# Hand-set order on all engines, eight 64x32 tiles for the state products, a transposed recurrent read and crossbar transposes in a cross-attention and ReGLU kernel

## The chip, the cores and the metric

The kernel runs on one core of a Trainium2 chip (trn2). The metric is the device time of one execution in microseconds (us); each figure is a median of several executions, and lower is better. A profile is one execution; its span, from the first to the last instruction, is about 1.8 us shorter than the time of the same execution.

The engines are called as the profile calls them: PE (matmuls), PEld (its weight loads), DVE (VectorE), ACT (ScalarE), POOL (GpSimd), SP (the engine that issues most DMAs here). "Crossbar transpose" is the name here for a transpose done by a DMA from one SBUF tile to another (DMA_TRANSPOSE in the traces). In these kernels the operands lie in SBUF, and PE leaves its products in PSUM, in pools of one-bank tiles, until ACT or DVE has read them.

## The reference, cut to what matters

Shapes: `x` is 8 batches of 8 heads, 512 tokens, 64 dimensions; `state` is 8 by 8 by 32 by 64. The feed-forward part has d_model 512 and d_ff 1536.

```python
scores = scale * x @ state^T                       # per batch and head: 512 x 32
a      = softmax(scores)                           # over the 32 states
xread  = a @ state                                 # 512 x 64
scores2 = scale * state @ x^T                      # the same products, transposed
a2     = softmax(scores2)                          # over the 512 tokens
sread  = a2 @ x                                    # "recurrent read": 32 x 64
X = concat([xread, sread], tokens).reshape(8 * 544, 512)
out = (relu(X @ w_gate) * (X @ w_val)) @ w_out     # 4352 x 512, float32
```

Both versions use one algebraic step: for the 512 tokens of a batch, `xread @ w_gate` equals `a @ (state @ w_gate)`. The kernel computes `U = state @ w` for each batch (the "state products", for gate and value), and then one "gate product" with the attention as the moving operand. Only 256 rows per batch (8 heads of 32 states) enter the contraction instead of 512.

## The kernel before: the parts that matter

Everything is in bf16 with float32 accumulation. PE's order is set by hand; the other engines are ordered by the scheduler (`engines={PE}`).

```python
ps_gv = pool("ps_gv", 6, PS)      # PSUM banks for state products, gate and value products
ps_o  = pool("ps_o", 1, PS)       # one bank for output products
ps_m  = pool("ps_m", 1, PS)       # one bank for all that attention needs
...
def x_trans_pe(b, j):             # x transposed on PE, 4 x 4 per batch, copied by ACT or DVE
    ps = ps_m.tile([128, NC, 128], BF16, name="xT_ps", tag="m")
    for c in range(NC):
        nc.tensor.transpose(ps[:, c], xb[b][:, c, 2*j:2*j+2]..., id128)
...
def att_sr(b, kc):                # recurrent read: 8 heads x 32 states on the output rows
    ps = ps_m.tile([128, 272], FP32, name="sr_ps", tag="m")
    for c in range(NC):           # every head against every head of the half: 128 x 256
        nc.tensor.matmul(ps[:, 0:256], e_sn[...], xb[...], ...)
        nc.tensor.matmul(ps[:, 256:257], e_sn[...], ones, ...)    # row sums
    rr = 1 / ps[:, 256:257]                                       # DVE, 128 x 1
    for j2 in range(2):           # keep the wanted blocks, scaled (DVE, 64 x 128)
        nc.vector.tensor_scalar_mul(out=sr_sb[...], in0=ps[...], scalar1=rr[...])
def att_srT(b): ...               # and back: two PE transposes, two copies
...
def u_unit(b, w, kc, lo, n):      # state products: two 128x64 tiles side by side
    for j2 in range(2):
        nc.tensor.matmul(ps[64*j2:64*j2+64, 0:n], stT[:, b, 2*kc+j2], wsb[:, 2*kc+j2, lo:lo+n])
...
for s in range(2, B):             # a steady stage: 12 steps
    for jf in range(12):
        gv(s, jf)                 # 4 gate/value products of 512 columns, then ReLU and multiply
        out_mms(...)              # 4 output products of batch s-2
        # at steps 1, 5, 9: a burst of state products for batch s+1
        # at the others: one attention unit of batch s+1
```

`stT` holds two heads' states with zeros in between (a 128x64 block with two 64x32 blocks on its diagonal), so half of each state product multiplies zeros.

The softmax here doesn't subtract the row's maximum and nothing guards it: scores larger than these inputs give would overflow.

## Time and profile before

| | before |
|---|---|
| median time | 289.81 us (289.37 to 290.25, 2 runs) |
| span of the profiled run | 287.0 us |
| PE busy | 249.4 us, 87% |
| first gate product on PE | 27.03 us |
| first ReLU of stage 2 (all batches in steady flow from here) | 80.72 us |
| one of five steady stages | 27.85 us |
| last ReLU of the state rows to the end | 26.6 us |

A useful clock for this kernel is the start of the ReLUs on ACT: there are twelve per batch, so the 25th starts stage 2, and each following dozen is one stage. The "end" line is counted from the last of them.

The page of the kernel before: engine shares, then busy tenths in 40 slices with the clock granted to PE, then the chain of work that ended last.

```profile
span 287.0 us, 4072 instructions
PE 249.4 (87%) x1562; PEld 123.4 (43%) x1584; DVE 159.9 (56%) x289; ACT 123.2 (43%) x231; POOL 23.2 (8%) x32
...
PE   7264968799599999989998999999999999997773
...
PEclk9655889799999999999999999999999999999999
...
PE 71%; DVE 14%; issue 5%; ACT 5%; DMA 3%; SPq 0%; ACTq 0%
```

A warning on the PEclk line, which bears on all pages here: the traces hold no clock event before the first change (6.40 us in this one), and the line shows full clock up to there. The warm-up matmuls start 0.43 us apart in this trace, and matmuls of the same 512 columns start 0.216 us apart where it records a clock of 1.00 (the four from 138.38 on, below), so PE in fact ran at half clock then.

PE is the bound in the middle (slices at 9), and it is not in most of the first dozen slices and in the last four. So there are three questions: how much PE work a stage has, how long the set-up is, and why the end is loose.

The set-up, on PE, in the timeline of before (columns: start, duration, engine, line, what, and in brackets the idle time before it with what released it):

```profile
7.74 0.40 PE L133 MATMUL xT_ps<-id_94,xb 128*128 128x128 bf16 x4 [0.98 <-ACT xb L119]
12.68 0.58 PE L133 MATMUL xT_ps<-id_94,xb 128*128 128x128 bf16 x4 [4.54 <-ACT xT L135]
13.78 0.58 PE L133 MATMUL xT_ps<-id_94,xb 128*128 128x128 bf16 x4 [0.52 <-DVE xT L137]
15.04 0.59 PE L133 MATMUL xT_ps<-id_94,xb 128*128 128x128 bf16 x4 [0.67 <-ACT xT L135]
```

Each group after the first waits for the copy of the group before, because they share the one `ps_m` bank.

A steady stage by engine, in the windows view (busy time and number of instructions; then the clock, the share of the DMA engines and GB/s), between two first ReLUs:

```profile
110.30:138.15 27.85, 27.00 (x176) 13.04 (x178) 18.78 (x33) 14.07 (x26) 2.03 (x2) 1.00 0.16 60
```

PE is busy for 27.00 of 27.85 us at full clock (1.00): only less PE work makes the stage shorter, apart from the 0.85 us that it idles. One burst of state products in it, in the timeline:

```profile
138.38 1.03 PE L252 MATMUL o_ps<-wo_sb,h_sb 128*128 128x512 bf16 x4
139.34 0.62 PE L206 MATMUL up<-wg_sb,stT 128*64 128x512 bf16 x4
139.79 0.60 PE L206 MATMUL up<-wv_sb,stT 128*64 128x512 bf16 x4
140.32 0.40 PE L133 MATMUL xT_ps<-id_94,xb 128*128 128x128 bf16 x4
```

Ends are modelled and matmuls overlap (the first line shows 1.03 us, and the second starts 0.96 us after it), so read starts. Four output products started at 138.38 hold PE for 0.86 us (four times 0.216); the transposes could then have started at 139.24 and started at 140.32. The burst costs 1.08 us.

Most of the idle 0.85 us is one wait, before the attention transposes:

```profile
126.51 1.23 DVE L158 TENSOR_TENSOR a_sn<-e_sn,rc 128x1024 bf16<-128x1024 bf16 x1
...
127.65 0.71 DVE L185 TENSOR_SCALAR sr_sb<-sr_ps,rr 64x128 bf16<-64x128 f32 x2
...
128.41 0.40 PE L165 MATMUL aT_ps<-id_94,a_sn 128*128 128x128 bf16 x4 [0.70 <-DVE sr_sb L185]
```

And the end, where output products alternate with copies out of a single bank:

```profile
262.07 2.75 PE L252 MATMUL o_ps<-wo_sb,h_sb 128*128 128x512 bf16 x11 [0.78 <-DVE o_sb L263]
265.49 2.75 PE L252 MATMUL o_ps<-wo_sb,h_sb 128*128 128x512 bf16 x12 [0.68 <-ACT o_sb L261]
```

### The profile page before, as it was taken

Reading aid. Unit: us, or ns where it says so; the run is one execution under the profiler, and the core shown is the slowest. Engines: PE = TensorE matmul, PEld = TensorE weight load, DVE = VectorE, ACT = ScalarE, POOL = GpSimd, SP = SyncE. Lnnn points to the kernel's source line nnn. Section 1 sums busy time; section 2 is a strip of 40 time slices with the busy share of each in tenths; the row PEclk is TensorE's granted clock in tenths of the full one; section 3 lists DMA queues with packets and bytes.
Section 4 is the critical chain, followed back from the end, with each engine's and each line's share of the span. In section 5 each row is a group of like instructions: output and inputs, shape, how many; then the busy total and the mean of one; then the engine's idle time right before and its main releaser. Section 6 shows DMA issues by size and latency. Waiting matters only on the chain.

```text
span 287.0 us, 4072 instructions
## 1 busy us (share of the span) xinstructions
PE 249.4 (87%) x1562; PEld 123.4 (43%) x1584; DVE 159.9 (56%) x289; ACT 123.2 (43%) x231; POOL 23.2 (8%) x32
## 2 busy tenths in 40 slices
PE   7264968799599999989998999999999999997773
PEld 3142423344244444444444444444445445664331
DVE  3244749477855866686568656765686444222010
ACT  2341746377264545545554555356544442221000
POOL 8302022200110020002000000000000000000000
PEclk9655889799999999999999999999999999999999
DMA  8999943440040115001011011001010011011112
GB/s 191 219 246 216 242 91 130 133 147 0 2 146 37 39 38 184 37 38 39 37 74 39 0 59 53 37 33 43 38 39 37 37 46 67 37 73 39 73 73 74
DMA packets 21235, 22.80 MB, mean 79 GB/s; under 512 B 3040, under 2 KB 16864, under 8 KB 21216
## 3 DMA queue, kind: packets, MB, share of 16 engines
q1 hardware_dynamic: 14176, 17.30, 18.0%
q0 software_dynamic: 5808, 4.72, 10.3%
q10 hardware_dynamic: 1232, 0.52, 0.8%
q8 instruction: 12, 0.20, 0.3%
q14 instruction: 7, 0.06, 0.1%
HBM read 18.35 MB, written 8.91 MB: 95 GB/s over the span
## 4 chain that ended last, share of the span: by engine, by line
PE 71%; DVE 14%; issue 5%; ACT 5%; DMA 3%; SPq 0%; ACTq 0%
PE o_ps L252 27%; PE gv_ps L227 24%; PE up L206 7%; PE gvs_ps L240 4%; PE xT_ps L133 3%; DVE h_sb L232 3%; DMA xf<-in_x_dram 3%; DVE sr_sb L185 2%; PE aT_ps L165 2%; PE sr_ps L176 2%; PE sc_ps L146 2%; DVE a_sn L158 2%; ACT e_sn L148 1%; DVE cs L154 1%; DVE UG L211 1%
## 5 line engine op out<-in xcount | busy, mean ns | idle before, releaser
L252 PE MATMUL o_ps<-wo_sb,h_sb 128*128 128x512 bf16 x363 | 94.0, 379 | 4.0 <-DVE o_sb L263 1.6
L232 DVE TENSOR_TENSOR h_sb<-gv_ps,g_sb 128x512 bf16<-128x512 f32 x96 | 66.2, 691 | 54.4 <-ACT g_sb L231 49.3
L231 ACT ACTIVATE g_sb<-gv_ps 128x512 bf16<-128x512 f32 x96 | 57.4, 598 | 52.6 <-PE gv_ps L227 46.7
L227 PE MATMUL gv_ps<-ans,UG 128*128 128x512 bf16 x192 | 59.3, 390 | 0.3 <-ACT ans L169 0.2
L227 PE MATMUL gv_ps<-ans,UV 128*128 128x512 bf16 x192 | 58.7, 387 | 0.3 <-DVE UV L211 0.3
L252 PEld LDWEIGHTS <-h_sb 128*128 128x128 bf16 x384 | 37.5, 98 | 46.6 <-issue 4.3
L227 PEld LDWEIGHTS <-UV 128*128 128x128 bf16 x192 | 19.0, 99 | 25.3 <-issue 1.8
L123 POOL CAST xb<-xf 128x1024 bf16<-128x1024 f32 x14 | 14.2, 1042 | 107.0 <-PE sr_ps L179 71.9
L209 ACT CAST UG<-up 128x512 bf16<-128x512 f32 (+1 forms) x26 | 14.4, 554 | 19.4 <-PE up L206 19.3
L211 DVE CAST UG<-up 128x512 bf16<-128x512 f32 (+1 forms) x26 | 16.7, 643 | 10.6 <-PE up L206 10.6
L133 PE MATMUL xT_ps<-id_94,xb 128*128 128x128 bf16 x128 | 13.0, 227 | 8.9 <-ACT xT L135 6.6
L227 PEld LDWEIGHTS <-UG 128*128 128x128 bf16 x192 | 15.3, 99 | 9.2 <-issue 2.5
L263 DVE COPY o_sb<-o_ps 128x512 f32<-128x512 f32 x16 | 11.1, 692 | 12.6 <-PE o_ps L252 12.6
L261 ACT COPY o_sb<-o_ps 128x512 f32<-128x512 f32 x16 | 9.4, 586 | 19.4 <-PE o_ps L252 19.4
L133 PEld LDWEIGHTS <-xb 128*128 128x128 bf16 x128 | 9.4, 101 | 17.0 <-issue 11.4
L211 DVE CAST UV<-up 128x512 bf16<-128x512 f32 (+1 forms) x26 | 16.6, 640 | 0.0
L206 PEld LDWEIGHTS <-stT 128*64 128x64 bf16 x208 | 10.4, 115 | 14.2 <-issue 9.4
L206 PE MATMUL up<-wg_sb,stT 128*64 128x512 bf16 (+1 forms) x104 | 16.4, 394 | 0.0
L206 PE MATMUL up<-wv_sb,stT 128*64 128x512 bf16 (+1 forms) x104 | 16.2, 394 | 0.0
L176 PE MATMUL sr_ps<-xb,e_sn 128*128 128x256 bf16 x64 | 11.7, 285 | 4.2 <-DVE sr_sb L185 3.5
L165 PE MATMUL aT_ps<-id_94,a_sn 128*128 128x128 bf16 x64 | 6.7, 231 | 9.5 <-DVE sr_sb L185 7.8
L209 ACT CAST UV<-up 128x512 bf16<-128x512 f32 (+1 forms) x26 | 14.5, 558 | 0.6 <-PE up L206 0.4
(53 smaller groups left out, 183.9 us busy)
## 6 DMA issues: line engine op xcount, KB each, us to landing
out_dram<-o_sb SPq DMA_DIRECT2D x32, 256.0 KB, 2.3
xf<-in_x_dram SPq DMA_DIRECT2D x7, 1024.0 KB, 5.6
wo_sb<-in_moe_w_out_dram POOLq DMA_DIRECT2D x3, 512.0 KB, 24.0
xf<-in_x_dram SPq DMA_DIRECT2D x2, 512.0 KB, 6.9
wg_sb<-in_moe_w_gate_dram POOLq DMA_DIRECT2D x2, 512.0 KB, 15.0
wv_sb<-in_moe_w_val_dram POOLq DMA_DIRECT2D x2, 512.0 KB, 17.8
wg_sb<-in_moe_w_gate_dram POOLq DMA_DIRECT2D x2, 256.0 KB, 8.3
wv_sb<-in_moe_w_val_dram POOLq DMA_DIRECT2D x2, 256.0 KB, 8.9
```

Source lines behind the costliest of these rows:

```text
L123: nc.gpsimd.tensor_copy(out=o, in_=s)
L133: nc.tensor.transpose(ps[:, c], xb[b][:, c, 2 * j:2 * j + 2].rearrange("p h d -> p (h d)"), id128)
L165: nc.tensor.transpose(ps[:, c], asn[b][:, c, 128 * kc:128 * kc + 128], id128)
L176: nc.tensor.matmul(ps[:, 0:256], e_sn[b][:, c, 4 * kc:4 * kc + 4].rearrange("p h n -> p (h n)"), xb[b][:, c, 4 * kc:4 * kc + 4].rearrange( ...
L206: nc.tensor.matmul(ps[64 * j2:64 * j2 + 64, 0:n], stT[:, b, 2 * kc + j2], wsb[:, 2 * kc + j2, lo:lo + n], start=True, stop=True)
L209: nc.scalar.copy(out=usb[:, kc, lo:lo + n], in_=ps[:, 0:n])
L211: nc.vector.tensor_copy(out=usb[:, kc, lo:lo + n], in_=ps[:, 0:n])
L227: nc.tensor.matmul(ps.rearrange("p (c t) -> p c t", c=NC), usb[:, kc, f0:f0 + 128], ANS[b][:, :, kc], start=(kc == 0), stop=(kc == 1))
L231: nc.scalar.activation(out=g_sb, in_=pss[0], func=AF.Relu)
L232: nc.vector.tensor_tensor(out=hsb[b][:, jf], in0=pss[1], in1=g_sb, op=ALU.mult)
L240: nc.tensor.matmul(ps[:, w], wsb[:, j, f0:f0 + 128], br[:, j].rearrange("p b n -> p (b n)"), start=(j == 0), stop=(j == NJ - 1))
L252: nc.tensor.matmul(o_ps[0], src[:, jf, tsub * 128:(tsub + 1) * 128], wo_sb[:, jf], start=(jf == 0), stop=(jf == NF - 1))
```

## The change

Its intent: take transposes and zeros off PE, and order all engines so that PE rarely waits. In parts:

1. **State products on eight 64x32 tiles.** The diagonal blocks of `stT` are multiplied alone, two row groups by four column groups of the array, meant to take the time of the zeros away (0.40 us per burst in E1). The state is put into this form by products with permutation matrices (`perm`) instead of transposes.
2. **Transposed recurrent read.** `xb` is the stationary operand now and the exponentials move, 64 columns at a time, so the result comes out as `br` needs it: no transposes, no copies; the sums come from products with ones.
3. **Crossbar transposes** for x and the attention of batches 2 to 7.
4. **PSUM**: six shared banks and two for the output products. The score products, for one, no longer share a single bank with everything else. (In SBUF, the buffer for the loaded x, `xin`, goes from one to two.)
5. **Order**: all engines by hand; batch 0 is loaded in four pieces and its attention is pipelined by head pairs; batch 0 and 1 gate products are spread so that four output pieces are done before stage 2; all eight small stores at the end go out on SP.

```diff
-    ps_gv = pool("ps_gv", 6, PS)
-    ps_o = pool("ps_o", 1, PS)
-    ps_m = pool("ps_m", 1, PS)
+    ps_r = pool("ps_r", 6, PS)
+    ps_o = pool("ps_o", 2, PS)
 # ... cut: loads and the form of the state
+    def x_bar(b):
+        nc.sync.dma_start_transpose(out=xT[b]..., in_=xb[b]...)
+    def a_bar(b):
+        nc.sync.dma_start_transpose(out=ANS[b]..., in_=asn[b]...)
 # ... cut: scores, softmax
+    def sr_mm(b):
+        ps = ps_r.tile([128, 2, NJ, 64], FP32, name="sr_ps", tag="r")
+        for c in range(NC):
+            for j in range(NJ):
+                nc.tensor.matmul(ps[:, 0, j], xb[b][:, c, 2*j:2*j+2]..., e_sn[b][:, c, 2*j:2*j+2]..., ...)
+        for c in range(NC):
+            for half in range(2):
+                for kc in range(2):      # sums, laid beside the wanted blocks
+                    nc.tensor.matmul(ps[:, 1, 2*kc:2*kc+2, 0:Ns], ones[:, half], ev[:, :, half ^ kc], ...)
+    def sr_ev(b):
+        nc.vector.reciprocal(out=rr, in_=ps[:, 1, :, 0:Ns])
+        # four DVE multiplies straight into br
+    def u_mms(b, ps, w, kc, lo, n, i):
+        for c in range(4):
+            r = (c + kc) % 2
+            j = 2 * kc + c // 2
+            s = c % 2
+            nc.tensor.matmul(ps[32*c:32*c+32, 0:n], stT[64*r:64*r+64, b, j, 32*s:32*s+32],
+                             wsb[w][64*r:64*r+64, j, lo:lo+n], ...)
 # ... cut
-    order = tc.manual_schedule(engines={mybir.EngineType.PE})
-    ctx.enter_context(order)
+    ctx.enter_context(tc.manual_schedule())
 # ... cut: the set-up, written out step by step
+    def aux(n, jf):                      # attention and state products of the next batch
+        if jf == 0:   sc_mm(n, 0); sc_exp(n, 0)
+        elif jf == 1: sc_mm(n, 1); sc_exp(n, 1)
+        elif jf == 2: nrm_sum(n); u_burst(n, 0, 512, "avav")
+        elif jf == 3: nrm_mul(n)
+        elif jf == 4: a_bar(n); sr_mm(n)
+        elif jf == 5: sr_ev(n); u_burst(n, 512, 512, "avav")
+        elif jf == 8: u_burst(n, 1024, 512, "avav")
+    def nxt(n, jf):                      # x of the batch after that
+        if jf == 6:   x_alloc(n); x_conv(n, 0, 4, "p")
+        elif jf == 7: x_conv(n, 4, 4, "p"); x_dma(n + 1)
+        elif jf == 9: x_bar(n)
 # ... cut
+    for s in range(2, B):
+        for jf in range(NF):
+            gv(s, jf); outp(); aux(s + 1, jf); nxt(s + 2, jf)
```

## The prediction

> **What bounds the kernel.** TensorE: the page gives it 249.4 of 287.0 us busy; the chain that ended last is 71% PE. By stretches: (a) 0 to 81.6 us, prologue, before batch 2's first gate product; in the busy table PE has 1.6, 4.7 and 3.6 us of 7.2 in the second to fourth slices, mostly at a granted clock of 0.5; the first gate product starts at 27.0; (b) five equal stages of 27.85 us, read from the ReLU starts on ACT (110.30, 138.15, 166.00, 193.85), PE busy 27.0, DVE 18.8, ACT 14.1; (c) two last stages, about 41 us; (d) 24.8 us of remaining output products and stores.
>
> **A stage of 27.85 us.** Without attention, one step (four gate/value, four output products of 512 columns) takes 1.73 us, twelve 20.7. The other 7.1 us, from step lengths in the timeline: three state-product bursts at 1.15 (0.86 streaming[...]) 3.45; x transposes 0.85; scores 0.45; recurrent read 1.0; attention transposes 0.45; srT 0.1; a 0.8 stall before the attention transposes, behind DVE.
>
> **After, per stage.** All transposes (1.4 us) and the 0.8 stall leave PE. A burst has 16 small matmuls, eight at a time: streaming falls from 0.86 to 0.43, but [...]twice the weight loads remain; I estimate 0.9 instead of 1.15. The transposed read has 32 matmuls of 64 columns; scores run at 0.029 us per matmul, so 0.92: no gain. Sum 20.7+2.7+0.45+0.92 = 24.8; with 0.5 for new waits 25.3, so 12.7 us over five stages. [...]
> DVE falls from about 19.7 to 18 us of work per stage: the reciprocal of 128 row sums costs about 1 us (estimate from 140 ns for 1, 343 for 32), replacing four 349 ns scalings.
>
> **Crossbar.** The 512 KB x transpose queues on SP behind a 1 MB load (5.6 us to landing). Both go out about step 8; scores need it 8 to 9 us later: little slack. [...] The attention transpose has about 16 us.
>
> **Prologue.** Batch 0's x comes in four pieces ahead of most of the state, and attention is pipelined by head pairs: first gate product at about 15 instead of 27. The 4 us stall near 73-76, waits behind single-buffered PSUM tiles and batch 2's PE transposes go. I sum 40 us of PE work from there, plus stalls and cold clock: stage 2 at about 62 instead of 81.6, with four output pieces done (3.45 us).
>
> **End.** 14 instead of 18 output pieces; double-buffered output PSUM removes most of 5.8 us of waits. Eight small stores all on SP: 1 us worse.
>
> **Sum.** 62 + 5x25.3 + 41.6 + 12.1 + 5.3 = 247.5 span, plus 2.8 (time less span before) and 2.7 for crossbar waits: 253 us, 244 to 266. Faster 0.96, within 2% 0.02, slower 0.02.
>
> **Right or wrong in the profile.** Stage period 25.3; length of steps with a burst; scores waiting on a DMA (crossbar late) or not; first gate product's and stage 2's start; PE idle before gate products (DVE late).
>
> **What would make it wrong.** Crossbar transposes slower than 8 us would stall every stage and hold stores and loads in SP's queue; weight loads of 32-column tiles not hidden; prologue limited by weight transfers (8 MB moved in the first 36 us).

## The result, and the profile after

A ratio below is the mean time of one kernel's runs over that of the other's of the same rounds, so it is not quite the ratio of the medians that are quoted.

| | before | after | difference |
|---|---|---|---|
| median time | 289.81 us | 247.01 us (245.25 to 248.77, 2 runs) | ratio 0.853 (0.838 to 0.868) |
| span of the profiled run | 287.0 | 243.4 | 43.6 |
| first gate product on PE | 27.03 | 18.23 | 8.8 |
| first ReLU of stage 2 | 80.72 | 61.56 | 19.2 |
| five stages | 139.3 | 123.4 | 15.9 |
| stage 7 and the state rows | 40.5 | 40.3 | 0.2 |
| last such ReLU to the end | 26.6 | 18.2 | 8.4 |

The five stages after are 25.90, 24.21, 24.19, 24.92 and 24.19 us. The same page lines of the kernel after:

```profile
span 243.4 us, 4462 instructions
PE 224.9 (92%) x1775; PEld 107.3 (44%) x1775; DVE 151.1 (62%) x267; ACT 112.0 (46%) x207; POOL 23.8 (10%) x34
...
PE   7477879999799999999999999999999999999991
...
PEclk9759999999999999999999999999999999999998
...
PE 79%; DMA 10%; DVE 6%; SPq 1%; ACT 1%; issue 1%; DVEq 0%
```

PE lost 24.5 us of busy time, and is at 9 from the seventh slice to the last but one, with one exception. In the chain, DVE went from 14% to 6% and DMA from 3% to 10%. An undisturbed stage, in the windows view, has no idle time on PE at all:

```profile
89.50:113.69 24.19, 24.19 (x194) 10.88 (x193) 17.13 (x28) 12.15 (x24) 2.02 (x2) 1.00 0.45 121
```

The burst of state products after, in the timeline:

```profile
104.32 1.03 PE L289 MATMUL o_ps<-wo_sb,h_sb 128*128 128x512 bf16 x4
105.28 0.41 PE L230 MATMUL u_ps<-wg_sb,stT 64*32 64x512 bf16 x8
105.50 0.40 PE L230 MATMUL u_ps<-wv_sb,stT 64*32 64x512 bf16 x8
105.84 1.04 PE L262 MATMUL gv_ps<-ans,U 128*128 128x512 bf16 x4
```

Read as before: the gate products could have started at 105.18 and started at 105.84. The burst costs 0.66 us in place of 1.08, and 0.56 in place of 0.98 from its first matmul on. Streaming was four rounds of 0.215 us and is two, which is 0.43 less; all else stayed at about 0.22 us.

The recurrent read after (16 products with x, 16 with ones) takes from 120.79 to 121.73, 0.94 us:

```profile
120.79 0.63 PE L201 MATMUL sr_ps<-e_sn,xb 128*128 128x64 bf16 x16
121.26 0.63 PE L209 MATMUL sr_ps<-e_sn,ones 128*128 128x64 bf16 x16
121.73 1.03 PE L262 MATMUL gv_ps<-ans,U 128*128 128x512 bf16 x4
```

The wait that the change brought: scores that wait for the crossbar transpose of x. Two of the stages are longer by it.

```profile
61.79 1.03 PE L289 MATMUL o_ps<-wo_sb,h_sb 128*128 128x512 bf16 x4
64.35 0.41 PE L156 MATMUL sc_ps<-stT,xT 128*128 128x64 bf16 x8 [1.53 <-DMA xT<-xb]
```

The set-up on PE, where before had groups of transposes waiting for copies:

```profile
13.86 0.41 PE L230 MATMUL u_ps<-wg_sb,stT 64*32 64x256 bf16 x8
...
15.10 3.20 PE L116 MATMUL stT_ps<-perm,st_b 128*64 128x256 bf16 x28 [0.61 <-DVE st_b L76]
18.23 1.51 PE L262 MATMUL gv_ps<-ans,U 128*128 128x512 bf16 x4
```

And the end, without a wait:

```profile
225.02 7.93 PE L289 MATMUL o_ps<-wo_sb,h_sb 128*128 128x512 bf16 x36
232.79 5.34 PE L289 MATMUL o_ps<-wo_sb,hs_sb 128*128 128x512 bf16 x24
```

### The profile page after: what moved, and what is told of

The parts are those of the page before. It is cut to its first block, busy times and chain, and to the rows that moved or that the text cites. A ratio compares the mean times of both kernels' runs of the same rounds, so it can differ in the third digit from the quotient of the medians.

```text
span 243.4 us, 4462 instructions
## 1 busy us (share of the span) xinstructions
PE 224.9 (92%) x1775; PEld 107.3 (44%) x1775; DVE 151.1 (62%) x267; ACT 112.0 (46%) x207; POOL 23.8 (10%) x34
## 4 chain that ended last, share of the span: by engine, by line
PE 79%; DMA 10%; DVE 6%; SPq 1%; ACT 1%; issue 1%; DVEq 0%
PE o_ps L289 33%; PE gv_ps L262 31%; DMA xT<-xb 5%; PE u_ps L230 5%; DMA st_f<-in_state_dram 5%; PE gvs_ps L275 4%; PE sc_ps L156 2%; PE sr_ps L209 2%; PE sr_ps L201 2%; DVE U L76 1%; PE stT_ps L116 1%; DVE h_sb L267 1%; SPq L89 1%; DVE rr L215 1%; DVE br L221 1%
## 5 line engine op out<-in xcount | busy, mean ns | idle before, releaser
L262 PE MATMUL gv_ps<-ans,U 128*128 128x512 bf16 x384 | 98.5, 381 | 3.0 <-DVE U L76 1.1
L262 PEld LDWEIGHTS <-U 128*128 128x128 bf16 x384 | 34.5, 98 | 48.7 <-issue 10.9
L74 ACT CAST U<-u_ps 128x512 bf16<-128x512 f32 x48 | 26.0, 590 | 19.0 <-PE u_ps L230 19.0
L76 DVE CAST U<-u_ps 128x512 bf16<-128x512 f32 x48 | 30.6, 676 | 2.9 <-PE u_ps L230 2.7
L74 ACT COPY o_sb<-o_ps 128x512 f32<-128x512 f32 (+1 forms) x18 | 10.1, 562 | 21.6 <-PE o_ps L289 21.6
L76 DVE COPY o_sb<-o_ps 128x512 f32<-128x512 f32 (+1 forms) x18 | 11.9, 659 | 10.8 <-PE o_ps L289 6.2
L230 PE MATMUL u_ps<-wv_sb,stT 64*32 64x512 bf16 (+1 forms) x208 | 11.2, 366 | 0.0
L181 DVE TENSOR_TENSOR a_sn<-e_sn,rc 128x1024 bf16<-128x1024 bf16 (+1 forms) x11 | 10.3, 938 | 0.1
L230 PE MATMUL u_ps<-wg_sb,stT 64*32 64x512 bf16 (+1 forms) x208 | 10.3, 374 | 0.0
L172 DVE TENSOR_REDUCE cs<-e_sn 128x32 f32<-128x1024 bf16 (+1 forms) x11 | 10.1, 919 | 0.0
## 6 DMA issues: line engine op xcount, KB each, us to landing
wo_sb<-in_moe_w_out_dram POOLq DMA_DIRECT2D x3, 512.0 KB, 25.3
```

The costliest lines, as they stand in the source:

```text
L74: nc.scalar.copy(out=o, in_=i)
L76: nc.vector.tensor_copy(out=o, in_=i)
L172: nc.vector.reduce_sum(out=c, in_=e, axis=AX.X)
L181: en.tensor_tensor(out=a, in0=e, in1=r.to_broadcast(list(e.shape)), op=ALU.mult)
L230: nc.tensor.matmul(ps[32 * c:32 * c + 32, 0:n], stT[64 * r:64 * r + 64, b, j, 32 * s:32 * s + 32], wsb[w][64 * r:64 * r + 64, j, lo:lo + n ...
L262: nc.tensor.matmul(ps.rearrange("p (c t) -> p c t", c=NC), U[b][:, kc, w, f0:f0 + 128], ANS[b][:, :, kc], start=(kc == 0), stop=(kc == 1))
```

## The experiments

Each takes the kernel after (or before, where said) and undoes or alters one part. Chips and rounds differ between the three groups of runs, so times are compared as ratios to before in the same rounds. "Costs 2%" means that the ratio of that kernel to before is 2% above the control's. All gave correct results. Stage lengths are those of the ReLU starts.

| run | median us | ratio to before (95%) | undisturbed stage us |
|---|---|---|---|
| c_after, the control | 246.28 | 0.850 (0.845 to 0.856) | 24.19 |
| e1_wide_tiles | 253.87 | 0.876 (0.872 to 0.880) | 25.39 |
| e2_four_at_a_time | 246.25 | 0.850 (0.846 to 0.854) | 24.21 |
| e2b_four_tiles | 253.00 | 0.874 (0.867 to 0.880) | 25.36 |
| e3_pe_transposes | 251.18 | 0.868 (0.863 to 0.872) | 25.53 |
| e4_old_read | 250.29 | 0.864 (0.860 to 0.869) | 24.80 |
| e5_only_pe_set | 253.19 | 0.875 (0.869 to 0.880) | 24.10 |
| e6_before_all_set (from before) | 293.17 | 1.012 (1.005 to 1.018) | 28.18 |
| e7_load_after | 242.85 | 0.838 (0.833 to 0.844) | 24.19 |
| e8_one_out_bank | 251.38 | 0.868 (0.864 to 0.873) | 24.27 |
| e9_front_whole | 247.99 | 0.856 (0.851 to 0.860) | 24.19 |
| b1_best | 240.53 | 0.829 (0.826 to 0.833) | 24.19 |

### The control: the kernel after, again

> The changed kernel unmodified, as a control on the same chip. 245 to 249 us, ratio to before 0.845 to 0.86; stage period 24.2 us; a state-product burst takes 0.56 us from its first matmul to the next gate product's.

It ran four times, 245.63 to 248.83 us. The profiled execution was the slowest, and shows where a part of the spread comes from. Its wait for the crossbar was 2.19 us, and after it the clock granted to PE fell, so that four gate products took 1.75 us instead of 1.03 (timeline, then windows of the same run):

```profile
65.61 0.41 PE L156 MATMUL sc_ps<-stT,xT 128*128 128x64 bf16 x8 [2.19 <-DMA xT<-xb]
65.85 1.75 PE L262 MATMUL gv_ps<-ans,U 128*128 128x512 bf16 x4
```

```profile
62.40:65.60 3.20, 1.01 (x5) 0.28 (x3) 0.69 (x1) 0.35 (x1) 2.02 (x2) 1.00 1.01 156
65.60:67.50 1.90, 1.89 (x13) 0.91 (x14) 0.00 (x0) 1.19 (x2) 0.00 (x0) 0.61 0.00 0
```

(The 0.61 is a mean over the stretch; with the 0.61 of 67.50 to 70.00 it fits a clock of 0.50 from about 66.0 to 69.4 us.) That stage took 28.23 us, 4.0 more than an undisturbed one, where the first profile of the same kernel had 25.90 with a wait of 1.53 us and the clock at 1.00. So here a wait of 2.19 us came with a loss of nearly twice its own length. It need not: the clock also fell after a wait of 2.0 us in E2b (0.72 over 66 to 72 us), and did not after one of 2.1 us in E4 (1.00 over 63 to 70 us), so the length of the wait alone does not decide. What does was not shown. All five stages of this profile took 126.4 us, 3.0 more than in the first.

### Are the 64x32 tiles worth what they promise?

E1 puts the state products back on two 128x64 tiles.

```diff
-        for c in range(4):
-            r = (c + kc) % 2
-            j = 2 * kc + c // 2
-            s = c % 2
-            nc.tensor.matmul(ps[32*c:32*c+32, 0:n], stT[64*r:64*r+64, b, j, 32*s:32*s+32], ...)
+        for j2 in range(2):
+            j = 2 * kc + j2
+            nc.tensor.matmul(ps[64*j2:64*j2+64, 0:n], stT[:, b, j], wsb[w][:, j, lo:lo+n], ...)
```

> Undoes only the 64x32 tiles: the state products run as before on two 128x64 tiles with the zero halves; everything else as in the changed kernel, the result is correct. Theory A (the burst is streaming plus a fixed price of about 0.2 us[...], weight loads hidden): each of the 22 bursts of 512 columns costs 0.43 us more, 4 of 256 columns 0.21 more, about 10 us in all: 256 to 258 us, stage period 25.5. Theory B (as predicted blind: twice as many weight loads eat most of it, 0.25 us a burst): 5 to 6 us: 252 to 253 us, stage period 24.9.

It costs 3.0%. The undisturbed stage is 25.39 us instead of 24.19: 1.20 us for three bursts, 0.40 each, close to the 0.43 of streaming that the tiles save. The five stages make 6 of some 7 us (3% of 247); the bursts of the set-up have only the rest. The time came out between the two theories; the stage, expected at 25.5 or 24.9 us, decides for the first.

E2 asks whether eight tiles really run at once, by changing the order of issue so that the same four tiles come twice in a row: gate A, value A, gate B, value B, where A and B are the two sets of four tiles.

```diff
-            for w in range(2):
-                for kc in range(2):
+            for kc in range(2):
+                for w in range(2):
```

> Same 64x32 tiles, same instructions, but issued so that four matmuls of one set of tiles are followed by four more of the same set, then the other set: at most four different tiles at a time. Theory A (the gain is eight tiles streaming at once): a burst streams 0.86 us again, time as with the wide tiles, 256 to 258 us, stage period about 25.5. Rival (the gain comes from halving the contraction or from the smaller weights, whatever the order): as the control, 246 to 248 us.

This missed: nothing changed (246.25 us, the same ratio). The trace shows why the experiment didn't do what it was meant to do. The program order on PE was four gate, four value, four gate, four value; the records show eight gate products, then eight value products (timeline, sorted by start):

```profile
105.95 0.42 PE L230 MATMUL u_ps<-wg_sb,stT 64*32 64x512 bf16 x8
106.18 0.41 PE L230 MATMUL u_ps<-wv_sb,stT 64*32 64x512 bf16 x8
```

The gate products of set B started ahead of the value products of set A that stand before them in the kernel's text: up to 106.00 us the timeline lists all eight gate products and no value product, and the first value products at 106.18. Set A's tiles had gate products from 105.95 on, and set B's had none before; that this is the reason is my reading. So in this run matmuls to different tiles did start out of program order, the four gate products of set B 0.2 us before value products that precede them in the text.

E2b therefore changes not the order but the number of tiles: every product goes to one of only four of the eight tiles (the heads are laid into other halves of the partitions, and the sums follow).

```diff
-            r = (c + kc) % 2
+            r = c % 2
 # and, to match, "half ^ kc" becomes "half" in perm, in the sums and in sr_ev
```

> The order experiment did not limit the tiles: its trace shows the four matmuls for the free set starting beside the first four. Here the limit is in the layout: heads are not swapped for the second half of the feature blocks, so both halves use the same four of the eight 64x32 tiles; same number and size of matmuls and loads, correct result. Theory A (eight tiles streaming at once are the gain): a burst streams four rounds of 0.215 us, 0.43 us more, stage period 25.4 as with the wide tiles, 253 to 255 us, ratio to before 0.873 to 0.88. Rival (halved contraction or small weights are the gain): 24.2 and 246 us, ratio 0.85.

It costs 2.7%, nearly as much as E1, and the stage is 25.36 us. Its burst:

```profile
104.89 0.61 PE L230 MATMUL u_ps<-wg_sb,stT 64*32 64x512 bf16 x8
105.33 0.60 PE L230 MATMUL u_ps<-wv_sb,stT 64*32 64x512 bf16 x8
105.87 1.04 PE L262 MATMUL gv_ps<-ans,U 128*128 128x512 bf16 x4
```

From 104.89 to 105.87 are 0.98 us, exactly the figure of before, although the tiles are 64x32 and the weight loads the same sixteen. So all that the small tiles gain comes from eight running at once, and sixteen weight loads cost no more than eight did: in E2's burst all sixteen together show 0.14 us of PEld time. The prediction had charged about 0.18 us per burst for them (0.9, less 1.15 with 0.43 of streaming taken off).

### The crossbar: what it takes off PE, and what its waits cost

E3 puts all transposes back on PE, with the new PSUM pools and order.

```diff
-    x_bar(2)
 # and in the stages
-            a_bar(n)
+        elif jf in (6, 7):
+            ps = a_tr(n, jf - 6)
+            a_ev(n, jf - 6, ps, "av"[jf - 6])
-        elif jf == 9:
-            x_bar(n)
+        elif jf >= 8:
+            ps = x_tr(n, jf - 8)
+            x_ev(n, jf - 8, ps, "av"[jf % 2])
```

> Undoes only the crossbar transposes: x and attention of batches 2 to 7 are transposed on PE again, with their PSUM copies on ACT and DVE, placed with slack (x at steps 8 to 11 of the stage before its scores, attention at steps 6 and 7). Theory D (the crossbar saves PE 1.3 us per batch and the 0.8 us stall was a matter of placement): stage period 25.4 to 25.6, no waits on xT, six batches cost 8 us and 3 to 5 us of waits on the crossbar go: 250 to 252 us, ratio 0.86 to 0.87. Rival (the stall and the PSUM waits come back with PE transposes): stage period 26.3 or more, 255 us or more.

It costs 2.0%. Four of its stages, with no waits, are 25.53 us, in the windows view all of it PE time; the fifth, which has no x left to transpose, is 24.63:

```profile
113.90:139.43 25.53, 25.53 (x218) 12.29 (x216) 18.23 (x31) 13.62 (x26) 1.95 (x3) 1.00 0.25 83
```

So the crossbar takes 1.34 us off each of four stages and 0.44 off the fifth, 5.8 us in five. In the profile after, the waits for it give back 2.5 us of that (1.71, 0.02, 0, 0.73 and 0 over the five stages, each its length less 24.19); in the control's slower execution, with the clock that it lost, they gave back 5.5, nearly all. That E3 has no idle PE time in a stage also shows that the wait of before ahead of the attention transposes can go without the crossbar.

E7 keeps the crossbar, and issues the x transpose of a batch before the 1 MB load of the next x instead of after it, on the same queue.

```diff
         elif jf == 7:
             x_conv(n, 4, 4, "p")
+            x_bar(n)
             if n + 1 < B:
                 x_dma(n + 1)
-        elif jf == 9:
-            x_bar(n)
```

> One line moved: on the SP queue the crossbar transpose of x goes out before the 1 MB load of the next batch, not behind it. Theory C (the scores' waits, 1.5 us in stage 2, 0.3 to 0.7 later, come from the load ahead in the queue): the PE waits on xT vanish, the transpose lands in about 3 to 4 us instead of 7.4, 2 to 3 us gained: 244 to 245 us where the control has 247. Rival (the crossbar itself is slow, 5 us for 512 KB whatever is ahead): the waits and the time stay as in the control.

It gains 1.4% over the control (0.838 to 0.850, the intervals apart), 3.5 us. The tile's view gives the issue time on SP (least, median, most, in ns) and the time from issue to landing. First the kernel after, then E7:

```profile
L147 SPq DMA_TRANSPOSE xT<-xb x6: 1431/4368/5577, 32.1 to 153.9; - x6
...
DMA to landing us min/median/max: 4.3/7.4/10.8
```

```profile
L147 SPq DMA_TRANSPOSE xT<-xb x6: 1423/1882/2111, 33.5 to 154.1; - x6
...
DMA to landing us min/median/max: 4.3/4.4/10.4
```

With no load ahead of it the transpose landed 4.4 us after its issue (median); the other 3 us of the 7.4 were the load. An earlier issue is not the reason: in the second steady stage it went out 17.85 us after the first ReLU of its stage, and 17.35 us in E7. In E7 no score waits for the crossbar, and all five stages are 24.19 us. (Its profiled execution was its slowest, 245.27 us, with a slower set-up at a lower clock; the other three were 241.81 to 242.97. B1 below has the same move with an early stage 2, at 60.66 us, and no such wait either.)

### The transposed read

E4 puts the old read back, with two banks from the pool of six and the old transposes and copies.

```diff
-        # 16 products with xb stationary, 16 with ones
+        for kc in range(2):
+            ps = ps_r.tile([128, 272], FP32, name="sr_ps", tag="r")
+            for c in range(NC):
+                nc.tensor.matmul(ps[:, 0:256], ev, xb[b][...], ...)
+                nc.tensor.matmul(ps[:, 256:257], ev, ones[:, 0, 0:1], ...)
 # reciprocal, four scalings into sr_sb; two PE transposes at step 7, copies into br
```

> Undoes only the transposed recurrent read: per batch 16 matmuls (256 columns and 1 column), 2 PE transposes, two small reciprocals, four scalings and four copies, as before the change. Theory E (predicted blind: no gain from the transposed read, 0.94 us on PE against about 1.0 to 1.1): 246 to 248 us, stage period 24.2 to 24.4. Rival (it is a real part of the gain): more than 3 us slower, stage period 24.8 or more.

It costs 1.6%, about 4 us; I had predicted that the transposed read gains nothing. The undisturbed stage is 24.80 us instead of 24.19, 0.61 us longer. The old read takes 1.08 us on PE instead of 0.94 (from 99.36 to 100.44 in E4's timeline), the transposes 0.11, and the rest is a wait of the gate products after the burst, for a bank that DVE still reads:

```profile
103.26 1.02 PE L269 MATMUL gv_ps<-ans,U 128*128 128x512 bf16 x4 [0.38 <-DVE sr_sb L217]
```

So 0.25 us is PE work and 0.38 us is how long DVE holds PSUM banks.

### The order: needed, or a gain of its own?

E5 is the kernel after with only PE's order set; the scheduler orders the rest.

```diff
-    ctx.enter_context(tc.manual_schedule())
+    ctx.enter_context(tc.manual_schedule(engines={mybir.EngineType.PE}))
```

> One argument: only PE's order is set by hand, as in the kernel before; the scheduler orders DVE, ACT, GpSimd and the SP queue. Theory F (PE bounds the kernel and its order is the same, so the order of the others is worth little): within 2 us of the control, 244 to 249 us. Rival (the set order on the others is a main part of the gain): 3 us or more slower, with PE waiting on DVE, ACT or DMA in the prologue or on xT.

This missed: it costs 2.8%, about 7 us, where 2 us at most were expected, and the set-up costs more than that: stage 2 starts at 74.24 us instead of 62.16 in the control. The scheduler put the eight small copies that make `perm` on DVE behind a cast that waits for the load of the state, and the first product with `perm` waited for it. DVE's timeline, then PE's:

```profile
15.35 0.63 DVE L76 CAST st_b<-st_f 128x896 bf16<-128x896 f32 x1 [3.86 <-DMA st_f<-in_state_dram]
15.89 0.95 DVE L109 COPY perm<-id 128x32 bf16<-128x32 bf16 x8
```

```profile
16.21 1.05 PE L116 MATMUL stT_ps<-perm,st_b 128*64 128x256 bf16 x4 [11.86 <-DVE perm L109]
```

In the stages the scheduler did a little better than the hand: 24.10 us each with no wait for the crossbar, 120.5 us for the five, against 123.4 in the first profile after. What the set order buys is the set-up.

E6 is the kernel before with every engine's order set, as its program text has it.

```diff
-    order = tc.manual_schedule(engines={mybir.EngineType.PE})
+    order = tc.manual_schedule()
```

> The kernel before with one argument changed: the order of all engines is set by the program, not only PE's. Theory G (the gain of the change does not lie in setting the order as such; the program's order is already close to what the scheduler chose): 285 to 295 us, ratio 0.98 to 1.02, stage period 27.5 to 28.5. Rival (the hand-set order is a main part of the gain): 280 us or less.

It is 1.2% slower than before, with stages of 28.18 instead of 27.85 us. Setting the order is no gain of its own; it is what lets the new set-up be written down.

### The end: the second output bank

E8 gives `ps_o` one bank again, and leaves the eighth unused.

```diff
-    ps_o = pool("ps_o", 2, PS)
+    ps_o = pool("ps_o", 1, PS)
```

> The changed kernel with one PSUM bank for the output product instead of two (the eighth bank stays unused). Theory H: the stages do not notice (a gate product stands between two output groups), stage period 24.2; at the end, where only output products are left, PE waits about 0.8 us for each of five evacuations: 4 us slower, 250 us, ratio 0.86 to 0.867. Rival (no cost, evacuation is hidden): 246 us, ratio 0.85.

It costs 2.1%. Its profiled span is 4.2 us longer than the control's, and 3.8 of them are at the end: 21.98 us from the last ReLU instead of 18.14. Four waits of before are back, two of which are:

```profile
235.98 2.75 PE L289 MATMUL o_ps<-wo_sb,h_sb 128*128 128x512 bf16 x12 [0.67 <-ACT o_sb L74]
239.51 2.75 PE L289 MATMUL o_ps<-wo_sb,hs_sb 128*128 128x512 bf16 x12 [0.78 <-DVE o_sb L76]
```

### The set-up: is it the loading in pieces?

E9 loads the whole state first and x in two halves, and does batch 0's attention in one piece, all else as after.

```diff
-    st_dma(0, 1)
-    for j in range(NJ):
-        x_dma(0, 2 * j, 2)
-    st_dma(1, B)
+    st_dma(0, B)
+    for j in range(2):
+        x_dma(0, 4 * j, 4)
 # and x_conv by halves, then all transposes, scores, exponentials, sums, multiplies in turn
```

> Undoes only the front of batch 0: the whole state is loaded first, x in two halves, and batch 0's attention is computed in one piece as batch 1's is, not by head pairs. Theory I (the front is most of the 8 us by which the first gate product moved ahead, and PE is busy behind it): first ReLU at 24 to 27 us instead of 18.7 to 19.3, everything behind it later by the same, 251 to 255 us, ratio 0.868 to 0.88. Rival (weights or batch 1's data bound the prologue, the lead is lost again): first ReLU late but stage 2 starts at 61 to 64 us as in the control, 246 to 248 us.

I had credited the pieces and head pairs with most of the earlier first gate product. The expectation, a first ReLU at 24 to 27 us, missed: it came at 20.14. The pieces are worth little: the ratio is 0.6% above the control's, with intervals that overlap (about 1.5 us, not resolved), and the first gate product comes at 19.50 instead of 18.23 us (17.88 to 18.59 over the control and E2, E7 and E8, which leave this front as it is). The rest of the lead of 8.8 us over before has another cause. (The windows view gives E9 a clock of 1.00 up to that product. But its eight attention transposes took 1.03 us at 14.36 and the same eight of the next batch 0.62 us at 35.38. In the kernel after, transposes start 107 ns apart at 11.5 us, where the clock is recorded as 0.50, and 56 ns apart at 6.3 us, where it is recorded as 1.00: for eight that is a difference of 0.36 us between starts. So E9 seems to have run this stretch at half clock, and the kernel after had 3.4 us of full clock in it, from 5.57 us on: E9 may overstate the pieces a little.)

### A version that beats both

B1 is E7 with three more moves: the last small stores on SP and ACT by turns; the DVE work of batch 0's read after the next burst rather than before it; two gate products of batch 0 moved into the wait before batch 1's attention transposes.

```diff
+                eng = nc.sync if bq % 2 == 0 else nc.scalar
-                nc.sync.dma_start(out=outr[tsub * 4 + bq, S:SP], ...)
+                eng.dma_start(out=outr[tsub * 4 + bq, S:SP], ...)
 # sr_ev(0) moved below u_burst(0, 256, ...); gv(0, 6) and gv(0, 7) moved above a_tr(1, ...)
 # x_bar(n) above x_dma(n + 1), as in E7
```

> A version meant to beat both: the crossbar transpose ahead of the load (as in the run with the load after), the last small stores split over the SP and ACT queues, the recurrent read's DVE work of batch 0 behind the first burst's evacuation instead of ahead of it, and two more gate products of batch 0 ahead of batch 1's attention transposes, where PE waited 1.4 us. Expected: no waits on xT, PE waits at 22 to 25 us and at 32 us gone or halved, tail 1 us shorter: 239 to 242 us, ratio 0.823 to 0.835. If the prologue is bound elsewhere: 242 us, ratio 0.837.

240.53 us (239.13 to 240.94, six runs), 0.829 of before. That is 2.5% faster than the control, by the ratio of the two ratios (0.8292 and 0.8504), with intervals apart. E7's part of it is shown. The other three moves would make 1% more (0.8292 against E7's 0.8381), but the intervals overlap by a little (0.833 and 0.8325), so that is not quite resolved, and the moves are not told apart; only the end can be read alone: from the last ReLU on it takes 17.25 us instead of 18.17, and the split stores are the one move that touches it.

## Why the prediction was right, and where it was not

The predicted time of 253 us lies 6 us above the measured 247, inside the range. In ReLU starts, the predicted span was 250.2 us with waits, and 243.4 came. The difference of 6.8 us (6.0 in time, since the median of the two runs lies 3.6 us above the profiled span and 2.8 had been added) is: stages 5.8, stage 7 and the state rows 1.3, the set-up 0.4, and the end 0.8 the other way. How far the runs explain the gain of 43.6 us differs by part: most of the stages and half of the end are tied to a part of the change by a run; of the 19.2 us of the set-up, only about 1.3 are.

- **The bound.** PE, 27.00 of 27.85 us in a stage, and less PE work is what made the stage shorter: right. It is 24.19 of 24.19 now.
- **A stage.** Predicted 25.3 us, measured 24.19 undisturbed. Of the 3.67 us saved, the experiments assign 1.17 to the bursts (E2b; E1 gives 1.20), 1.34 to the transposes (E3) and 0.61 to the read (E4). The 0.55 left is about the wait before the attention transposes, which measured 0.70 us before and had been taken as 0.8; that this is its place was argued from the trace, not isolated. The parts were undone one at a time, and that they add up is assumed.
- **The bursts: the mis-sized term.** That streaming halves was right, 0.86 to 0.43 us. Beyond its streaming a burst costs about 0.22 us before (1.08 less 0.86) and after (0.66 less 0.43), with 128x64 and with 64x32 tiles; what this time goes into was not shown. The size was off: "twice the weight loads remain; I estimate 0.9 instead of 1.15". It was 1.08, and it is 0.66. The weight loads of the small tiles did not add to it (0.14 us of PEld time for sixteen in E2's burst), and E2b, with the same loads and half of the tiles at once, loses the gain. Over fifteen bursts, 0.66 instead of 0.9 makes 3.6 of the 5.8 us.
- **The allowance of 0.5 us per stage for new waits** makes another 2.5 us: none were there in undisturbed stages, since the crossbar waits had a term of their own. DVE has 17.1 us of work in 24.19 (predicted 18) and doesn't hold PE up. (3.6 and 2.5 are 0.3 too much: the other steps of a stage are about 0.1 us longer than predicted, and the crossbar waits 0.2 shorter in all.)
- **The transposed read.** "so 0.92: no gain": the length was right (0.94), the conclusion wrong. E4 shows 0.61 us per stage. Of it 0.25 us is PE work (0.14 in the read and 0.11 in transposes that I had counted with the others), and 0.38 us is a bank held by DVE, which no sum of PE work shows. The sum of the prediction holds all the same, as it was made from the lengths after, not from savings. The estimate of 1 us for the reciprocal was good (0.95).
- **The crossbar waits.** Predicted 2.7 us, measured 2.5 in the first profile and 5.5 in the control's, with the clock that it lost; so the close agreement is partly luck. The cause given was right: the transpose queues behind a 1 MB load (7.4 us to landing, and 4.4 in E7, median). The 512 KB transpose alone takes those 4.4 us from issue to landing with no load ahead of it.
- **The set-up.** Stage 2 was predicted at 62 us and its first gate product came at 60.9. That agreement is luck: the start failed, and the stretch behind it was over-estimated by as much (47 us implied, from 15 to 62, and 42.7 measured). The step failed in its reason: "first gate product at about 15 instead of 27" by pieces and head pairs. It came at 18.2, and E9 shows that the pieces give only about 1.3 us of it. What gave the rest was not isolated. In the trace of before, the 5.7 us from the end of the first bursts to the attention transposes (19.8 to 25.5) are the recurrent read with its waits on DVE, which after comes behind the gate products; and the single bank for attention makes PE wait for each copy, 4.54 us in one place, where that copy on ACT stood behind another that waited for DVE, and DVE for the second half of x. Both are argued, not tested, and so is the second x buffer; this stays open.
- **From there to stage 2** (27.03 to 80.09 before, 18.23 to 60.93 after, in the windows view), 10.4 us went, of which 5.8 were idle time of PE (10.4 to 4.5) and 4.5 busy time, although four output pieces of 0.86 us were added. This fits the removed stall and transposes that the prediction named, and a clock of 0.99 instead of 0.90, but no run takes these apart.
- **The end.** 18.17 us. Four pieces fewer are 3.45 us, the second bank 3.8 (E8), the remaining 1.1 is not assigned. That all small stores on SP would cost 1 us agrees with B1, the only kernel that splits them: its end is 0.9 us shorter.
- **The set order** is not a term of the sum. E5 and E6 show that it was right to leave it out of the stages, and that the new set-up needs it: 12 us would have been lost there.

## What to carry to other kernels

When many small matmuls replace large ones, count how many tiles of the array work at the same time, and check it by halving that number: here the gain came from eight at once (0.56 us from a burst's first matmul on, and 0.98 with four), and sixteen weight loads cost no more than eight did. Try a transpose moved from PE to a DMA ahead of the bulk load on its queue (E7: 4.4 us to landing instead of 7.4, and 3.5 us less time), and measure its landing time, since a wait that PE sees may come with a lower clock (in the control, 2.19 us of wait and then 0.61 over the next 1.90 us). Before crediting a gain to a new schedule, undo one part at a time: the order, the pieces and the banks looked like one thing, and the runs gave them 12 (7 in the whole time), about 1.5 and 4 us.
